# Four early jobs from a one-row slot list, scatters queued behind the next decay, and deeper x and v buffers in a retention + mixture-of-experts kernel

## The chip, the cores and the metric

One core of a Trainium2 chip runs the whole kernel. The metric is the device time of one execution in microseconds. The profile shows one execution, with the span from its first to its last instruction and the tensor clock that was granted.

## The reference

Retention with one state per head (4 sequences, 8 heads, 768 steps, width 64), then a mixture of experts over the 3072 tokens (width 512, 8 experts, hidden width 1024) in which each token goes to its best expert only:

```
state = gamma[h] * state + k_t v_t^T ;  y_t = scale * q_t state        # for t in 0..767
x = y as [3072, 512]
logits = x @ w_gate + modality_bias[modality_id];  e = argmax(logits)
gate = softmax(logits)[e]
out[token] = gate * (relu(x @ w1[e]) @ w2[e])
```

## The kernel before

**Retention.** Each sequence is cut into 6 chunks of 128 steps, so there are 24 chunks, numbered n. In chunk form y = (masked q k^T) v plus q times the state so far; the decay is folded into v (`decay_v`, on POOL) and into the output (`decay_q`, on ACT, used by DVE in `yT`). One chunk is four quarters, between which the generator `retention(n)` yields:

- loads are queued on SP, then the hooks "top", `decay_v(n+1)`, the update of the state `st`, and the hooks "st";
- `scores(n+1)` and the hooks "sc";
- the hooks "pr", `tokens_out(n-1)` (transpose of y and the gate logits; the result goes to a tile `xs`) and the hooks "tk";
- `heads_out(n)` and the hooks "end".

PE, ACT, DVE and SP run their instructions in the order of the program text. POOL's decays and index fills are pinned to that order as well.

**Routing.** After each group of three chunks, `route_a` (softmax parts, one-hot `oh`, running counts `cnt`) and `route_b` (rank of each token within its expert by matmuls, then the row number `pos`) give each token a row in `xsl`, a table in HBM with one region of 3072 rows per expert. `scatter` writes a chunk's 128 rows of x there by an indirect DMA on POOL. An `xs` tile comes free when its scatter has landed; there are 4. `setup_stores` writes 512 empty rows at the end of the table.

**Slots and jobs.** Each expert's region is divided into slots of 512 rows, 48 in all. A job is the two-layer network on one slot with its expert's weights: `rows_in` reads the slot's rows, `ids` takes token numbers and gates, `flip` transposes the rows, `raw` loads and `cut` splits the weights into a high and a low part, and 32 steps of 6 matmuls follow (`first`: 16 steps for h, `second`: 16 for o). Outputs are scattered to their tokens by POOL. While job k runs, hooks load and prepare job k+1.

Jobs come from lists. An *early* list is made while retention still runs, from slots that are already full: with `EARLY = (3, 5)` one list after 9 chunks and one after 15. `early_a` to `early_e` rank all 48 slots in a 48 x 48 comparison, with PE matmuls that broadcast the counts (`pce`, L388), pick the winner (`pte`) and mark it as taken (`ptk`). The *final* list (`final_a` to `final_d`, matmuls `pcf` and `ptf`) ranks what is left after all 24 chunks; `gaps_*` and `gap` then fill the unused rows of half-filled slots with zeros, by nine indirect DMAs on POOL (L583), before the final jobs' rows are read. Two slots of at most 32 tokens are computed as small "rests" inside later jobs. A loop at the end of the kernel takes any slots that are left over.

**The order.** Chunks 0 to 13 run alone (`FIRST_JOB = 14`). From then on job steps and quarters of chunks alternate, two quarters after an even step, one after an odd step. When retention is over, `last_tokens` runs piece by piece; each `PAUSE` hands one job step to PE. The six jobs are e0, e1 (early), f0 to f3 (final).

Of the kernel before, what the change touches and what calls it, by code (L numbers as in the profile page):

```python
# [15 lines left out]
P = 128  # L16
# [24 lines left out]
FIRST_JOB = 14  # L41
# [9 lines left out]
def kernel(  # L51
# [52 lines left out]
    cnd = cp.tile([NCAND, NCAND + 4], F32, name="cnd")  # L104
# [88 lines left out]
    def tokens_out(n, yT):  # L193
        gr = n // GRP
        if n % GRP == 0:
            lg[gr] = sm.tile([P, GRP, NE], F32, tag="lg", name=f"lg_{gr}")
        xs = xss[n] = wk.tile([P, NG, P + NE], F32, tag="xs", name=f"xs_{n}", bufs=4)
        for u in range(2):
            px = bank(f"x_{n}_{u}")[:, : 2 * (P + NE)].rearrange("p (g e) -> p g e", g=2)
            for g in range(2):  # L200
                nc.tensor.matmul(  # L201
                    px[:, g], yT[:, 2 * u + g], wgt[:, 2 * u + g], start=(g == 0), stop=(g == 1),
                    skip_group_check=True,
                )
            nc.scalar.copy(xs[:, 2 * u : 2 * u + 2], px)  # L205
# [77 lines left out]
    def route_a(gr, part):  # L283
# [10 lines left out]
        elif part == 1:  # L294
            l, ex = mid[gr]
            eq = sm.tile(shp, F32, tag="eq", name=f"eq_{gr}")
            nc.vector.scalar_tensor_tensor(eq, l, 0.0, iota3m, op0=ALU.is_equal, op1=ALU.mult)
            mn = sm.tile([P, GRP], F32, tag="mn", name=f"mn_{gr}")
            nc.vector.tensor_reduce(mn, eq, axis=AX.X, op=ALU.min)
            oh = sm.tile(shp, BF16, tag="oh", name=f"oh_{gr}")  # L300
            nc.vector.tensor_tensor(
                oh, iota3m, mn.unsqueeze(2).to_broadcast(shp), op=ALU.is_equal
            )
# [12 lines left out]
    def route_b(gr):
        oh, _ = mid.pop(gr)
# [17 lines left out]
        mid[gr] = pos  # L335
# [33 lines left out]
    def list_consts():  # L369
# [8 lines left out]
        bias = small("bias", [1, 2])  # L378
        nc.vector.memset(bias, 0.0)
        nc.vector.memset(bias[:, 0:1], float(EMPTY))  # L380
        lc.update(ord_r=ord_r, vals=vals, bias=bias)
# [35 lines left out]
    def early_a(k):  # L417
        mid["e"] = ranks_a(f"e{k}", cnt[EARLY[k]])

    def early_b(k):  # L420
        szr, szc = mid["e"]
        mid["e"] = (ranks_b(f"e{k}", szr, szc, lists.get("taken")), szc)

    def early_c(k):

        rank, szc = mid["e"]
        hit = small(f"hit{k}", [NCAND, 1])
        nc.vector.tensor_scalar(hit, szc, float(SLOT), None, op0=ALU.is_ge)
        nc.vector.scalar_tensor_tensor(hit, rank, 0.0, hit, op0=ALU.is_equal, op1=ALU.mult)
        if "taken" in lists:  # L430
# [3 lines left out]
        pick = small(f"pick{k}", [NCAND, 2], BF16)
        nc.vector.tensor_scalar(pick, lc["vals"], hit, None, op0=ALU.mult)
        mid["e"] = (hit, pick)

    def early_d(k):
        hit, pick = mid["e"]
        pt = bank(f"pte{k}")  # L440
        nc.tensor.matmul(pt[:1, 0:2], ones[:NCAND, :1], pick, start=True, stop=True)
        lst = small(f"lst{k}", [1, 2], I32)
        nc.vector.tensor_tensor(lst, pt[:1, 0:2], lc["bias"], op=ALU.add)
        lists[k] = lst
        dg = small(f"dg{k}", [NCAND, NCAND], BF16)
        nc.vector.tensor_scalar(dg, ident[:NCAND, :NCAND], hit, BIG, op0=ALU.mult, op1=ALU.mult)
        mid["e"] = (hit, dg)

    def early_e(k):
        hit, dg = mid.pop("e")  # L450
        pk = bank(f"ptk{k}")
        nc.tensor.matmul(pk[:NCAND, :NCAND], ones[:NCAND, :NCAND], dg, start=True, stop=True)
        tkr = small(f"tkr{k}", [NCAND, NCAND])
        tkc = small(f"tkc{k}", [NCAND, 1])
        if "taken" in lists:
            was = lists["taken"]
            nc.vector.tensor_tensor(tkr, pk[:NCAND, :NCAND], was[0], op=ALU.add)
            nc.vector.scalar_tensor_tensor(tkc, hit, BIG, was[1], op0=ALU.mult, op1=ALU.add)
        else:
            nc.vector.tensor_copy(tkr, pk[:NCAND, :NCAND])  # L460
            nc.vector.tensor_scalar(tkc, hit, BIG, None, op0=ALU.mult)
        lists["taken"] = (tkr, tkc)
# [351 lines left out]
    for g in range(NGRP - 1):  # L814
        t = (g + 1) * GRP
        if g + 1 in EARLY:
            k = EARLY.index(g + 1)
            at(t, "end", route_a, g, 0)
            at(t, "end", route_a, g, 1)
            at(t + 1, "sc", route_a, g, 2)  # L820
            at(t + 1, "sc", route_b, g)
            at(t + 1, "sc", early_a, k)
            at(t + 1, "pr", scatter, g, 0)
            at(t + 1, "end", scatter, g, 1)
            at(t + 2, "st", scatter, g, 2)
            at(t + 1, "pr", early_b, k)
            at(t + 1, "end", early_c, k)
            at(t + 2, "sc", early_d, k)
            at(t + 2, "pr", place_early, k)
            at(t + 3, "sc", early_e, k)  # L830
        else:
            at(t, "end", route_a, g, 0)
            at(t + 1, "st", route_a, g, 1)
            at(t + 1, "sc", route_a, g, 2)
            at(t + 1, "sc", route_b, g)
            for i in range(GRP):
                at(min(t + 1 + i, NN - 1), "pr", scatter, g, i)

    t = EARLY[0] * GRP + 2
    e = jobs[0]  # L840
    at(t, "tk", two, raw, e, 1, (0, 1))
    at(t, "end", two, raw, e, 1, (2, 3))
    at(t + 1, "pr", rows_in, e)
    at(t + 2, "top", ids, e)
    at(t + 1, "end", cut, e, 1, 0)
# [41 lines left out]

    def last_tokens():
        tokens_out(NN - 1, carry["y"])
        yield PAUSE  # L890
        route_a(NGRP - 1, 0)
        yield PAUSE
        route_a(NGRP - 1, 1)
        yield PAUSE
        final_a()
        route_a(NGRP - 1, 2)
        yield PAUSE
        route_b(NGRP - 1)
        final_b()
        scatter(NGRP - 1, 0)  # L900
        yield PAUSE
        gaps_a()
        scatter(NGRP - 1, 1)
        yield PAUSE
        final_c()
        gaps_b()
        scatter(NGRP - 1, 2)
        gaps_room()
        yield PAUSE
        final_d()  # L910
# [57 lines left out]
    with tc.manual_schedule(engines={PE, ACT, DVE, SP}):  # L968
# [16 lines left out]
        at(4, "top", setup_stores)  # L985
# [39 lines left out]
def _layout(inputs):  # L1025
# [37 lines left out]
    cand = np.zeros((NCAND, NCAND + 4), f)  # L1063
# [57 lines left out]
```

## Time and profile before

| | |
|---|---|
| runs | 451.58 us median of 3 (450.89 to 453.02) |
| profiled execution | 452.26 us |
| its span | 450.3 us |
| mean granted clock | 0.959 |
| busy: PE, DVE, ACT, POOL | 405.9, 201.0, 156.4, 92.3 us |
| DMA | 82.31 MB, mean 183 GB/s |

The span is divided into 40 slices of 11.26 us, in each of which a digit gives the busy tenths of an engine; slices are counted from 0. PE is TensorE's matmuls, PEld its weight loads, DVE VectorE, ACT ScalarE, POOL GpSimd, SP the queue that issues most DMAs. A row of a timeline has the start, the length, the engine, the line and the tiles written and read; in brackets is the idle time before it and what ended that. DMA share is the mean busy share of the 16 DMA engines.

### The profile page before, as it was taken

How to read it: one execution, taken by the hardware profiler on the slowest of the kernel's cores; microseconds unless marked ns; L12 is line 12 of the kernel's file. 1: busy time of each engine (PE TensorE's matmuls, PEld its weight loads, DVE VectorE, ACT ScalarE, POOL GpSimd, SP SyncE). 2: the span in 40 equal slices, each digit the busy share in tenths (PEclk: the TensorE clock that was granted, in tenths of full speed). 3: DMA queues.
4: the chain of work that ended last, by engine and by line, in shares of the span. 5: the costliest groups of instructions: out<-in, count | busy, mean ns of one | idle time of the engine just before them, and what ended most of it. 6: DMA issues, size and time to landing. Idle time of an engine off the chain costs nothing.

```text
span 450.3 us, 8319 instructions
## 1 busy us (share of the span) xinstructions
PE 405.9 (90%) x3104; PEld 331.3 (74%) x3104; DVE 201.0 (45%) x509; ACT 156.4 (35%) x309; POOL 92.3 (20%) x116
## 2 busy tenths in 40 slices
PE   4995959299799999999479999999999999999994
PEld 4874848188587787878368888887888888878883
DVE  1682565366765755477242146214352346224200
ACT  1541342236342454323222335223342334224211
POOL 2304414021041221357301100110001000100011
PEclk9998988879989999999869999999999999999998
DMA  8988655938548832334562347952534279810011
GB/s 283 336 226 284 203 204 182 359 151 298 172 146 295 278 118 91 150 143 172 179 206 103 131 153 284 335 193 58 189 116 144 114 233 310 305 73 0 2 47 43
DMA packets 30490, 82.31 MB, mean 183 GB/s; under 512 B 5485, under 2 KB 5613, under 8 KB 30193
## 3 DMA queue, kind: packets, MB, share of 16 engines
q1 hardware_dynamic: 25024, 66.10, 44.2%
q0 software_dynamic: 5136, 15.21, 8.5%
q8 instruction: 26, 0.43, 0.4%
q10 hardware_dynamic: 288, 0.44, 0.3%
q14 instruction: 16, 0.13, 0.1%
HBM read 65.42 MB, written 23.41 MB: 197 GB/s over the span
## 4 chain that ended last, share of the span: by engine, by line
PE 51%; issue 13%; DVE 3%; POOL 2%; DMA 2%; ACT 1%; POOLq 0%; SPq 0%; DVEq 0%; ACTq 0%
PE h_f L657 15%; PE o_f L675 14%; PE o_e L675 9%; PE h_e L657 3%; PE x L201 2%; PE xp_f L642 2%; PE y L183 2%; PE sc L159 1%; POOL xsl L583 1%; DMA xsl<-kqr,run_pos 1%; DMA xg_f<-xsl 1%; DVE lo_e L636 1%; POOL out_dram L683 1%; PE y L177 1%; PE st L215 1%
## 5 line engine op out<-in xcount | busy, mean ns | idle before, releaser
L636 DVE TENSOR_TENSOR lo_f<-raw_f,hi_f 128x1024 fp32r<-128x1024 f32 x32 | 39.2, 1225 | 49.8 <-ACT hi_f L634 49.8
L665 DVE SCALAR_TENSOR_TENSOR hTl_f<-h_f,hTh_f 128x512 fp32r<-128x512 f32 x32 | 22.1, 692 | 67.1 <-ACT hTh_f L664 67.1
L657 PE MATMUL h_f<-xTh_f,hi_f 128*128 128x512 f32 x128 | 50.9, 397 | 0.0
L675 PE MATMUL o_f<-hi_f,hTh_f 128*128 128x512 f32 x128 | 50.3, 393 | 0.0
L657 PE MATMUL h_f<-xTh_f,lo_f 128*128 128x512 f32 x128 | 50.1, 391 | 0.0
L657 PE MATMUL h_f<-xTl_f,hi_f 128*128 128x512 f32 x128 | 50.0, 391 | 0.0
L675 PE MATMUL o_f<-lo_f,hTh_f 128*128 128x512 f32 x128 | 49.9, 389 | 0.0
L675 PE MATMUL o_f<-hi_f,hTl_f 128*128 128x512 f32 x128 | 49.8, 389 | 0.0
L683 POOL DMA_INDIRECT out_dram<-o_f,tok_f x16 | 15.5, 969 | 132.8 <-ACT o_f L682 113.8
L147 POOL TENSOR_TENSOR vd<-vt,cst 128x512 f32<-128x512 f32 x24 | 25.0, 1044 | 74.9 <-PE y L183 48.1
L164 DVE TENSOR_TENSOR a<-sc,cst 128x512 f32<-128x512 f32 x48 | 30.8, 684 | 20.4 <-PE sc L159 20.4
L664 ACT ACTIVATE hTh_f<-h_f 128x512 fp32r<-128x512 f32 x32 | 19.2, 599 | 55.9 <-PE h_f L657 55.9
L345 POOL DMA_INDIRECT xsl<-xs,pos x24 | 25.6, 1066 | 58.6 <-DVE xTl_e L648 9.1
L201 PE MATMUL x<-wgt,yT 128*128 128x136 f32 x192 | 30.9, 309 | 5.5 <-DVE yT L190 5.5
L205 ACT COPY xs<-x 128x272 f32<-128x272 f32 x48 | 18.2, 387 | 49.3 <-PE x L201 18.3
L159 PE MATMUL sc<-kqr 64*128 64x128 f32 x384 | 30.8, 304 | 5.0 <-DMA kqr<-in_qkv_dram 4.9
L634 ACT CAST hi_f<-raw_f 128x1024 fp32r<-128x1024 f32 x32 | 33.4, 1043 | 0.0
L201 PEld LDWEIGHTS x<-wgt,yT 128*128 128x128 f32 x192 | 27.3, 209 | 7.4 <-DVE yT L190 3.4
L159 PEld LDWEIGHTS sc<-kqr 64*128 64x128 f32 x384 | 25.9, 205 | 9.3 <-DMA kqr<-in_qkv_dram 5.1
L682 ACT ACTIVATE o_f<-o_f,gate_f 128x512 f32<-128x512 f32 x16 | 11.0, 688 | 59.9 <-issue 34.1
L657 PEld LDWEIGHTS h_f<-xTh_f,hi_f 128*128 128x128 f32 x128 | 24.0, 188 | 6.2 <-issue 1.2
L183 PE MATMUL y<-a,vd 128*64 128x128 f32 x384 | 28.4, 294 | 0.0
(191 smaller groups left out, 710.4 us busy)
## 6 DMA issues: line engine op xcount, KB each, us to landing
raw_f<-in_w_dram SPq DMA_DIRECT2D x32, 512.0 KB, 3.4
kqr<-in_qkv_dram SPq DMA_DIRECT2D x23, 512.0 KB, 6.0
raw_e<-in_w_dram SPq DMA_DIRECT2D x16, 512.0 KB, 5.1
vt<-in_qkv_dram SPq DMA_DIRECT2D x24, 256.0 KB
kt<-in_qkv_dram SPq DMA_DIRECT2D x20, 256.0 KB, 6.4
xg_f<-xsl SPq DMA_DIRECT2D x16, 272.0 KB, 4.1
kqr<-in_w_dram SPq DMA_DIRECT2D x8, 512.0 KB
xg_e<-xsl SPq DMA_DIRECT2D x8, 272.0 KB, 6.6
```

Source lines behind the costliest of these rows:

```text
L147: nc.gpsimd.tensor_tensor(vds[n], vv, dec[:, n % NCH].unsqueeze(2).to_broadcast([P, H, D]), op=ALU.mult)
L159: nc.tensor.matmul(pe[j][:, g * P : (g + 1) * P], kt[r, g], qt[r, g], start=True, stop=True, skip_group_check=True,)
L164: nc.vector.tensor_tensor(a[:, j], pe[j].rearrange("p (h t) -> p h t", t=P), mask.unsqueeze(1).to_broadcast([P, NG, P]), op=ALU.mult,)
L183: nc.tensor.matmul(py[j][g % 2 * D : (g % 2 + 1) * D, g // 2], vd[:, 2 * g + j], a[:, j, g], start=(s is None and g < 2), stop=(g >= 2), s ...
L201: nc.tensor.matmul(px[:, g], yT[:, 2 * u + g], wgt[:, 2 * u + g], start=(g == 0), stop=(g == 1), skip_group_check=True,)
L345: ins = nc.gpsimd.indirect_dma_start(out=xsl[:, :], out_offset=bass.IndirectOffsetOnAxis(ap=mid[gr][:, i : i + 1], axis=0), in_=xs.rearran ...
L634: nc.scalar.copy(hi, t)
L636: nc.vector.tensor_tensor(lo, t, hi.bitcast(F32), op=ALU.subtract)
L657: nc.tensor.matmul(s.ph, s.w[1][f // 2][wi][:, o : o + P], s.xT[kc][a], start=(kc == 0 and k == 0), stop=(kc == KC - 1 and k == 2),)
L665: nc.vector.scalar_tensor_tensor(lo, s.ph, 0.0, hi.bitcast(F32), op0=ALU.max, op1=ALU.subtract)
L675: nc.tensor.matmul(s.po, s.hT[f][a][:, hh * P : (hh + 1) * P], s.w[2][f // 2][wi][:, (f % 2) * DM : (f % 2 + 1) * DM], start=(f == 0 and k ...
L683: ins = nc.gpsimd.indirect_dma_start(out=out[:, :], out_offset=bass.IndirectOffsetOnAxis(ap=s.tok[:, hh : hh + 1], axis=0), in_=o[:, :], i ...
```

## The change

- Four early jobs instead of two: lists after 9, 15 and 21 chunks, the last of which picks two. Two final jobs remain instead of four.
- An early list is made on one row of 48 slots instead of 48 x 48. A matmul sums the counts onto one partition; DVE marks the full slots, multiplies by a fixed priority (`bid`), takes the maximum, decodes slot and expert from it by a shift and a mask, and clears that slot's `bid`. The marks of taken slots for the final list are made once, from `bid` (`taken_a`, `taken_b`).
- `route_b` is divided: `route_c` holds its DVE part. For group g let t be chunk 3(g + 1). `route_a` 0 and 1 run at the end of chunk t; `route_b`, the list, `route_c` and `route_a` 2 now all run at the end of chunk t + 1 (they began in the middle of it); the scatters run in chunks t + 2 and t + 3, each after that chunk's decay (before: from chunk t + 1 on).
- Five `xs` tiles instead of four, three `vt` instead of two (v is loaded three chunks ahead), one `dq` instead of two.
- `setup_stores` moves from chunk 4 to chunk 7 and is declared independent of the scatters.
- The first job starts at chunk 15, and e0's loads, rows and flips are moved with it. `last_tokens` has 7 pauses instead of 9, with the gap stores ahead of `final_d`.

```diff
-EARLY = (3, 5)
-NEARLY = len(EARLY)
-NLAST = 4
+EARLY = {3: (0,), 5: (1,), 7: (2, 3)}
+NEARLY = 4
+NLAST = 2
-FIRST_JOB = 14
+FIRST_JOB = 15
...
-        t = vts[n] = ld.tile([P, DM], F32, tag="vt", name=f"vt_{n}", bufs=2)
+        t = vts[n] = ld.tile([P, DM], F32, tag="vt", name=f"vt_{n}", bufs=3)
-        t = wk.tile([P, NG, P], F32, tag="dq", name=f"dq_{n}")
+        t = wk.tile([P, NG, P], F32, tag="dq", name=f"dq_{n}", bufs=1)
-        xs = xss[n] = wk.tile([P, NG, P + NE], F32, tag="xs", name=f"xs_{n}", bufs=4)
+        xs = xss[n] = wk.tile([P, NG, P + NE], F32, tag="xs", name=f"xs_{n}", bufs=5)
...
-            nc.sync.dma_start(xsl[r : r + P, :], fill["none"])
+            ins = nc.sync.dma_start(xsl[r : r + P, :], fill["none"])
+            tc.add_to_no_dep_group("rows", ins.ins)
...
-    def early_a(k): ... early_e(k): ...        # 48 x 48 ranks, three matmuls
+    def early_a(g):
+        pt = bank(f"pte{g}")
+        nc.tensor.matmul(
+            pt[:1, :NCAND], ones[:, :1], cnt[g].unsqueeze(2).to_broadcast([P, NE, SPE]),
+            start=True, stop=True,
+        )
+        mid["e"] = pt
+    def early_b(g):
+        full = small(f"full{g}", [1, NCAND])
+        nc.vector.tensor_tensor(full, mid.pop("e")[:1, :NCAND], lc["full_at"], op=ALU.is_ge)
+        for k in EARLY[g]:
+            bid = lc["bid"]
+            key = small(f"key{k}", [1, NCAND])
+            nc.vector.tensor_tensor(key, full, bid, op=ALU.mult)
+            top = small(f"top{k}", [1, 1])
+            nc.vector.tensor_reduce(top, key, axis=AX.X, op=ALU.max)
+            num = small(f"num{k}", [1, 1], I32)
+            nc.vector.tensor_scalar(
+                num, top, -1.0, float(EMPTY * NE), op0=ALU.mult, op1=ALU.add
+            )
+            lst = small(f"lst{k}", [1, 2], I32)
+            nc.vector.tensor_scalar(lst[:, 0:1], num, 3, None, op0=ALU.logical_shift_right)
+            nc.vector.tensor_scalar(lst[:, 1:2], num, NE - 1, None, op0=ALU.bitwise_and)
+            lists[k] = lst
+            hit = small(f"hit{k}", [1, NCAND])
...
+                hit, key, top, full, op0=ALU.is_equal, op1=ALU.mult
...
+                bid, hit, 0.0, bid, op0=ALU.is_equal, op1=ALU.mult
+    def taken_a():
+        tk = small("tk", [1, NCAND], BF16)
+        nc.vector.tensor_scalar(tk, lc["bid"], 0.0, BIG, op0=ALU.is_equal, op1=ALU.mult)
+    def taken_b():
+        nc.tensor.matmul(pk[:NCAND, :NCAND], ones[:1, :NCAND], tk, start=True, stop=True)
+        nc.tensor.matmul(pk[:NCAND, P : P + 1], tk, ones[:1, :1], start=True, stop=True)
...
+        at(t, "end", route_a, g, 0)
+        at(t, "end", route_a, g, 1)
+        at(t + 1, "end", route_b, g)
         if g + 1 in EARLY:
...
+            at(t + 1, "end", early_a, g + 1)
+            at(t + 1, "end", early_b, g + 1)
+            for k in EARLY[g + 1]:
+                at(t + 2, "st", place_early, k)
...
+        at(t + 1, "end", route_c, g)
+        at(t + 1, "end", route_a, g, 2)
+        at(t + 2, "st", scatter, g, 0)
+        at(t + 2, "end", scatter, g, 1)
+        at(min(t + 3, NN - 1), "end" if t + 3 == NN else "st", scatter, g, 2)
+    t = GRP * min(EARLY)
     e = jobs[0]
...
+    at(t + 2, "sc", two, raw, e, 1, (0, 1))
+    at(t + 2, "end", two, raw, e, 1, (2, 3))
+    at(t + 4, "sc", rows_in, e)
+    at(t + 4, "end", cut, e, 1, 0)
+    at(t + 5, "top", raw, e, 2, 0)
+    at(t + 5, "sc", ids, e)
     for kc in range(KC):
+        at(t + 5, ("sc", "pr", "tk", "end")[kc], flip, e, kc)
...
-        if n + 2 < NN:
-            load_v(n + 2)
         if n + 3 < NN:
+            load_v(n + 3)
             load_kq(n + 3)
...
+        taken_a()
         yield PAUSE
+        route_a(g, 0)
+        taken_b()
         yield PAUSE
+        route_a(g, 1)
         yield PAUSE
+        route_b(g)
         final_a()
+        gaps_a()
+        route_c(g)
+        route_a(g, 2)
+        scatter(g, 0)
         yield PAUSE
         final_b()
+        gaps_b()
+        scatter(g, 1)
+        scatter(g, 2)
+        gaps_room()
         yield PAUSE
         final_c()
         gaps_c()
         for e in range(-1, NE):
             gap(e)
         yield PAUSE
+        final_d()
+        for i in range(NLAST):
             place(jobs[NEARLY + i], lists["final"], i, U + i)
...
-        at(4, "top", setup_stores)
+        at(7, "top", setup_stores)
```

More of the change, by code (lines that the diff above doesn't have):

```diff
@@ L103 @@
     ones = cp.tile([P, P], BF16, name="ones")
-    cnd = cp.tile([NCAND, NCAND + 4], F32, name="cnd")
+    cnd = cp.tile([NCAND, 2 * NCAND + 3], F32, name="cnd")
     cnt = [cp.tile([P, NE], BF16, name=f"cnt{i}") for i in range(NGRP + 1)]
@@ L308, in route_a @@
         else:
-            oh, ex = mid[gr]
+            pos, ex = mid[gr]
             den = sm.tile([P, GRP], F32, tag="den", name=f"den_{gr}")
@@ L314, in route_a @@
                 nc.vector.reciprocal(xss[gr * GRP + i][:, 0, P + 1 : P + 2], den[:, i : i + 1])
+            mid[gr] = pos
     def route_b(gr):
-        oh, _ = mid.pop(gr)
+        oh, ex = mid[gr]
         pr = bank(f"rk_{gr}")[:, : GRP * NE].rearrange("p (c e) -> p c e", e=NE)
@@ L329, in route_b, with route_c @@
             )
+        mid[gr] = (oh, ex, pr)
+    def route_c(gr):
+        oh, ex, pr = mid[gr]
         rk = sm.tile(shp, F32, tag="rk", name=f"rkt_{gr}")
@@ L334, in route_b @@
             nc.vector.tensor_reduce(pos, rk, axis=AX.X, op=ALU.add)
-        mid[gr] = pos
+        mid[gr] = (pos, ex)
     def scatter(gr, i):
@@ L377, in list_consts @@
         nc.vector.tensor_copy(vals[:, 1:2], ex_c)
[L378 to L381, printed above, removed]
+        full_at = small("full_at", [1, NCAND])
+        nc.vector.tensor_scalar(full_at, off_r[:1], float(SLOT), None, op0=ALU.add)
+        bid = small("bid", [1, NCAND])
+        nc.vector.tensor_copy(bid, cnd[:1, NCAND + 3 :])
+        lc.update(ord_r=ord_r, vals=vals, full_at=full_at, bid=bid)
     def ranks_a(t, counts):
@@ L415, in ranks_b @@
         return rank
[L417 to L430, printed above, removed]
+    def early_a(g):
[5 more added lines that the diff above has]
+        mid["e"] = pt
@@ L431, in early_c @@
             nc.vector.scalar_tensor_tensor(
-                hit, lists["taken"][1], 0.0, hit, op0=ALU.is_equal, op1=ALU.mult
+                hit, key, top, full, op0=ALU.is_equal, op1=ALU.mult
             )
[L434 to L461, printed above, removed]
+            nc.vector.scalar_tensor_tensor(
+                bid, hit, 0.0, bid, op0=ALU.is_equal, op1=ALU.mult
+            )
@@ new lines, in taken_a @@
+    def taken_a():
+        tk = small("tk", [1, NCAND], BF16)
+        nc.vector.tensor_scalar(tk, lc["bid"], 0.0, BIG, op0=ALU.is_equal, op1=ALU.mult)
+        lists["tk"] = tk
+    def taken_b():
+        tk = lists["tk"]
+        pk = bank("ptk")
+        nc.tensor.matmul(pk[:NCAND, :NCAND], ones[:1, :NCAND], tk, start=True, stop=True)
+        nc.tensor.matmul(pk[:NCAND, P : P + 1], tk, ones[:1, :1], start=True, stop=True)
+        tkr = small("tkr", [NCAND, NCAND])
+        nc.vector.tensor_copy(tkr, pk[:NCAND, :NCAND])
+        tkc = small("tkc", [NCAND, 1])
+        nc.vector.tensor_copy(tkc, pk[:NCAND, P : P + 1])
@@ L723, in rest_load @@
             for h in range(2):
-                t = ld.tile([P, DM], F32, tag=tag, name=f"rw{m}{i}{h}", bufs=2)
+                t = ld.tile([P, DM], F32, tag=tag, name=f"rw{m}{i}{h}", bufs=2 if k == 6 else 3)
                 nc.sync.dma_start(t, src[:, h * DM : (h + 1) * DM])
@@ L728, in rest_in @@
     def rest_in(s):
-        s.xg = wk.tile([P, XW], F32, tag="xs", name="rx", bufs=4)
+        s.xg = wk.tile([P, XW], F32, tag="xs", name="rx", bufs=5)
         for g in range(4):
@@ L815 @@
         t = (g + 1) * GRP
+        at(t, "end", route_a, g, 0)
+        at(t, "end", route_a, g, 1)
+        at(t + 1, "end", route_b, g)
         if g + 1 in EARLY:
[L817 to L839, printed above, removed]
-    e = jobs[0]
[L841 to L845, printed above, removed]
+            at(t + 1, "end", early_a, g + 1)
[8 more added lines that the diff above has]
+    t = GRP * min(EARLY)
+    e = jobs[0]
+    at(t + 2, "sc", two, raw, e, 1, (0, 1))
[4 more added lines that the diff above has]
+    at(t + 5, "sc", ids, e)
     for kc in range(KC):
-        at(t + 2, ("st", "sc", "tk", "end")[kc], flip, e, kc)
-    at(t + 2, "top", raw, e, 2, 0)
+        at(t + 5, ("sc", "pr", "tk", "end")[kc], flip, e, kc)
     carry = {}
@@ L888, in last_tokens @@
     def last_tokens():
+        g = NGRP - 1
         tokens_out(NN - 1, carry["y"])
+        taken_a()
         yield PAUSE
-        route_a(NGRP - 1, 0)
+        route_a(g, 0)
+        taken_b()
         yield PAUSE
-        route_a(NGRP - 1, 1)
+        route_a(g, 1)
         yield PAUSE
+        route_b(g)
         final_a()
-        route_a(NGRP - 1, 2)
+        gaps_a()
+        route_c(g)
+        route_a(g, 2)
+        scatter(g, 0)
         yield PAUSE
-        route_b(NGRP - 1)
         final_b()
[L900 to L903, printed above, removed]
+        gaps_b()
+        scatter(g, 1)
+        scatter(g, 2)
+        gaps_room()
         yield PAUSE
         final_c()
[L906 to L910, printed above, removed]
         gaps_c()
@@ L913, in last_tokens @@
             gap(e)
-        place(jobs[NEARLY], lists["final"], 0, U)
         yield PAUSE
-        for i in range(1, NLAST):
+        final_d()
+        for i in range(NLAST):
             place(jobs[NEARLY + i], lists["final"], i, U + i)
@@ L978 @@
         load_kq(2)
+        load_v(2)
         decay_v(0)
@@ L1062, in _layout @@
     ci = np.arange(NCAND)
[L1063 removed]
+    cand = np.zeros((NCAND, 2 * NCAND + 3), f)
     cand[:, :NCAND] = (ci % SPE) * SLOT
```

1 line of the change is left out of this document (added).

## The prediction

> **What bounds the kernel now.** I read the page's slices first, then the list of who waits for whom, filtered to PE, then busy time by stretches, then the timelines of PE, POOL, ACT and SP around each hole.
>
> ```profile
> PE 405.9 (90%) x3104; PEld 331.3 (74%) x3104; DVE 201.0 (45%) x509; ACT 156.4 (35%) x309; POOL 92.3 (20%) x116
> PE   4995959299799999999479999999999999999994
> PEclk9998988879989999999869999999999999999998
> ```
>
> PE is the bound, with 44.4 us idle out of 450.3. The slices put the holes before slice 11 (124 us) and at slice 19; slices 21 to 38 are full. The change can therefore win only in the first 100 us, around 120 us and around 220 us, and only up to those holes plus what the clock loses behind them.
>
> ```profile
> PE xp_e L642 <- DMA xg_e<-xsl: 8.6, 3, 8.2
> PE xp_f L642 <- DMA xg_f<-xsl: 8.6, 4, 6.3
> PE x L201 <- DVE yT L190: 5.5, 3, 3.3
> PE pce L388 <- DVE crepe L385: 5.4, 2, 3.2
> 58.60:62.00 3.40, 3.40 (x32) 2.82 (x32) 1.27 (x3) 1.18 (x4) 0.00 (x0) 0.50 0.39 156
> 88.80:96.10 7.30, 6.68 (x37) 5.33 (x38) 4.90 (x24) 1.56 (x3) 0.00 (x0) 0.50 0.67 262
> 123.40:126.80 3.40, 3.40 (x14) 3.10 (x15) 1.72 (x11) 0.77 (x2) 2.17 (x3) 0.51 0.23 87
> 222.40:229.00 6.60, 1.40 (x3) 0.55 (x3) 0.65 (x6) 0.00 (x0) 0.00 (x0) 0.50 0.78 233
> 229.00:232.60 3.60, 3.52 (x11) 3.04 (x12) 2.19 (x5) 2.12 (x3) 0.00 (x0) 0.50 0.46 181
> 232.70:444.00 211.30, 211.30 (x1119) 172.50 (x1117) 71.04 (x106) 70.86 (x104) 20.36 (x21) 1.00 0.43 152
> ```
>
> The waits (us, times, longest) name the holes: rows of the first early job, rows of the first final job, yT, and the early list's count. In the stretches (length, then busy time of PE, PEld, DVE, ACT, POOL, then granted clock, DMA share, GB/s) the clock is 0.50 behind each hole and 1.00 elsewhere: half of the busy time there is lost as well. From 232.7 on nothing can be won.
>
> **The change, part by part.** Sums are made against the profiled execution, 452.26 us: span 450.3 and 1.96 around it. It lies 0.7 above the median of 451.58.
>
> *Chunks 0 to 14, before any job.* Undisturbed, PE needs 4.30 us a chunk (12.43 to 25.34 is three):
>
> ```profile
> 11.77 0.63 PE L215 MATMUL st<-vd,kt 128*64 128x64 f32 x16
> 12.43 1.16 PE L159 MATMUL sc<-kqr 64*128 64x128 f32 x16
> 25.34 1.16 PE L159 MATMUL sc<-kqr 64*128 64x128 f32 x16
> 27.25 0.19 PE L319 MATMUL rk<-oh,upper 128*128 128x24 bf16 x1 [0.75 <-DVE oh L301]
> 27.57 1.17 PE L201 MATMUL x<-wgt,yT 128*128 128x136 f32 x8
> 33.82 1.17 POOL L345 DMA_INDIRECT xsl<-xs,pos  x1 [7.74 <-PE y L183]
> 36.43 1.02 POOL L345 DMA_INDIRECT xsl<-xs,pos  x1 [0.28 <-POOL xs L341]
> 39.85 0.67 ACT L205 COPY xs<-x 128x272 f32<-128x272 f32 x2 [9.52 <-DMA xsl<-xs,pos]
> 43.72 0.67 ACT L205 COPY xs<-x 128x272 f32<-128x272 f32 x2 [2.91 <-DMA xsl<-xs,pos]
> ```
>
> The first scatter stands on POOL until 33.8, after the four stores of empty rows (L248), with the next decay behind it; ACT's copy of x then waits for a free xs buffer, that is, for the scatter four chunks back to land, 6.0 to 7.3 us after it starts (33.82 to 39.85, 36.43 to 43.72). The stores lose that order and move to chunk 7; the scatters go behind the decay; a fifth xs gives each copy a chunk more. Chunk n's copy may start 4.3 us after its host chunk begins before PE feels it (two copies, lg and yT follow, then x). A scatter now starts about 1.5 us into the chunk before, so it lands 7.5 to 8.8 in, against 8.6 allowed: no wait in an ordinary group. Behind the list at 9 chunks, pos is about 1.3 us later and chunk 12's x may wait 1 to 2 us; that lies inside the wait for rows below. route_b now follows one-hots a chunk old, so waits like the 0.75 before rk go. The third v tile deepens a prefetch and costs nothing. One dq tile instead of two makes ACT wait for yT of the chunk before, which DVE does first in a chunk (0.86 us): covered, and if DVE lags, ACT lags with it.
>
> So chunk 14 is reached at 11.77 + 13 x 4.30, less four parts of 0.63 (two chunks without a state, two that start a sequence), plus four ranks of 0.32 (27.25 to 27.57): 66.4; state and scores (0.63, 1.16) end at 68.2, where PE wants e0's rows. When do they land? In the trace:
>
> ```profile
> 76.40 3.07 SPq L629 DMA_DIRECT2D raw_e<-in_w_dram  x4
> 81.18 2.47 SPq L612 DMA_DIRECT2D xg_e<-xsl  x4
> 90.81 0.48 PE L642 MATMUL xp_e<-cst,xg_e 128*128 128x128 f32 x1 [0.21 <-DMA xg_e<-xsl]
> 91.21 2.08 PE L159 MATMUL sc<-kqr 64*128 64x128 f32 x16
> 98.79 0.48 PE L657 MATMUL h_e<-xTh_e,hi_e 128*128 128x512 f32 x1
> 80.00:90.00 10.00, 1.58 (x22) 0.89 (x18) 2.77 (x10) 2.61 (x7) 1.12 (x2) 0.80 1.00 353
> ```
>
> Full DMA (share 1.00) moves 353 GB/s. A chunk is 512, 256 and 256 KB, a weight tile 512, a row tile or scatter 272. At 81.2 some 1.4 MB were queued (2.1 MB of weights and 1.05 of a chunk, less 4.8 us of work), plus 1.1 of rows: 7.1 us and about 2 for completion, and the last tile came 9.6 after the issue. The same reckoning after: the weights go out at chunks 11 and 12 (54 to 58 us), rows_in must wait for the scatter of chunk 8, which starts behind the decay of chunk 12 (59.9) and lands near 67. From 54 to 67 the queues are given three chunks (3.15), weights (2.1), three scatters (0.84): 6.1 MB; 12.9 us at 345 (353, a little less with scatters between) move 4.45. Backlog 1.65 and rows 1.1 take 8 us, completion 2: the last tile is there at 77. **PE again waits about 8 us for rows**, now at the flips of chunk 14. From the last tile to e0's first matmul the trace takes 8.0 (90.81 to 98.79), of which 2.4 are scores and ranks (91.21: 2.08; 0.32) that now lie ahead of the wait: e0 starts at 82.6. Today it starts at 98.79 with chunk 14 still to do, 4.3: **gain 20.5**. Bounds: 28 if the rows come before 68.2 (four flips at 0.87, the rest of the chunk 4.30 - 0.63 - 1.16, so 74.2), 13 if the weights' backlog, the stores at chunk 7 (1.1 MB) and the scatters add 7 us.
>
> *Early lists.* The old list holds PE at L388 from inside the chunk; the second costs 3.15 of wait (the 3.2 in the list of waits), 0.2, and half of 3.4 at clock 0.51. The new one is a matmul that PE passes without waiting and 8 small DVE operations for one job, 15 for two:
>
> ```profile
> 74.51 0.14 DVE L443 TENSOR_TENSOR lst<-pte,bias 1x2 int32<-1x2 f32 x1
> ```
>
> At 0.14, or a little more for 48 values, that is 1.3 and 2.4 us, on a DVE 45% busy, with pos and the next a behind it, neither due within 2 us. SP waits for the list at the end of chunk t+2's state, with nothing urgent behind it. **Gain 5.0**; bounds 3 and 5.5.
>
> *The final list.* With four early jobs, the list, the gap stores and the reads behind them belong to e2, one job later than f0 relative to their start.
>
> ```profile
> 187.87 1.17 PE x L201 x8
> 193.12 0.13 PE pcf L388
> 196.00 0.18 DVE L334 TENSOR_REDUCE pos<-rkt 128x3 int32<-128x24 f32 x1
> 196.50 0.48 PE L657 MATMUL h_e<-xTh_e,hi_e 128*128 128x512 f32 x1
> 198.20 0.19 PE ptf L490
> 205.10 0.98 POOL L583 DMA_INDIRECT xsl<-kqr,one_pos  x1 [0.88 <-DVE far_r L574]
> 222.68 2.10 SPq L612 DMA_DIRECT2D xg_f<-xsl  x4
> 225.38 0.15 DVE L623 COPY tok_f<-xg_f 128x1 int32<-128x1 int32 x1 [4.93 <-DMA xg_f<-xsl]
> 254.22 21.92 PE h_f L657 x96
> 276.14 0.87 PE xp_f L642 x8
> ```
>
> The hole here is 8.6 of wait and half of 1.40 + 3.52 at clock 0.50: 11.1 in all. After: retention ends at step 24 of e0 instead of 26 (36 quarters at 1.5 a step), so the last x ends seven steps of 1.37 (21.92 for 16) before e1. Call that end t (189.04 today). The work that had seven steps now has five: PE asks for pcf at t+4.3, three steps on, and for ptf two steps later, while today 5.1 us lie between the two (193.12, 198.20), with DVE at work on the keys and picks. I put 0.7 of PE wait before pcf and 1.3 before ptf: 2.0 new. e1 starts at t+11.9 and wants e2's rows after 16 steps, t+33.8. POOL gets pos at about t+6.7 (today t+7.1), does today's work (196.18 to 205.10 less 0.88 idle: 8.0) and starts the gaps at t+14.7; today 17.6 us pass until the rows are issued (205.10 to 222.68), 2.7 more to the first tile: t+35.0. PE waits 1.2, then the 2.3 between tiles (8.6 - 6.3). **Removed 11.1; added 2.0, 3.5 and one stretch at half clock, 1.7: gain 3.9.** Bounds: 9 (gaps land in time) and 0.
>
> Of that 1.7: rows show a wait of about 2 us followed by a half-clock stretch (2.07 before x at 58.28, then 58.6 to 62.0 at 0.50).
>
> ```profile
> 58.28 1.86 PE L201 MATMUL x<-wgt,yT 128*128 128x136 f32 x8 [2.07 <-DVE yT L190]
> ```
>
> The Trainium skill, page "TensorE: Matmul & The Clock Gate", Part 1, has the clock fall to half only after an idle window of about 3.4 us, free-running. By that rule a wait cut into 1.2 and 2.3 us would leave the clock alone and the sum would be 1.7 lower; this trace disagrees, and the row decides.
>
> *What stays.* Six job bodies and both rests, flips, outputs: moved, not changed. Routing the reference's inputs gives 5 full slots, one of 478, one of 31, one of 3; after 9, 15 and 21 chunks 2, 2 and 4 are full. All four early picks succeed, two final jobs take the full slot and the 478, and the loop at the end runs no turn, as today.
>
> **Sum:** 452.3 - 20.5 - 5.0 - 3.9 = 422.9 for a profiled execution, 422 for the median.
>
> **Rivals.** *The rows come in time:* the wait of 8.2 and that for e2's rows vanish, PE bounds from chunk 1 on: gains 28, 5.5, 9, so 409. For it: slices 11 to 18 show the same loads hidden. Against it: DMA share 1.00 in the row from 80 to 90. *New waits take more:* the backlog before chunk 14 and a DVE behind its lists; gains 13, 3, 0: 436. For it: the same full DMA row, at a slower pace than the new one. *DMA is the bound of the whole first phase*, and packing retention denser only moves the wait: gains 0, 3, 0, so 449. Against it: 18 chunks (18.1 MB: three carry no k), 11 scatters (3.1), stores (1.1), weights (2.6), rows (1.1) and constants are under 27 MB, 76 us at 353; today's phase is 99. *An early list finds no full slot* (the change fails its aim; slower): a job body runs on empty rows, 47 us (192 matmuls at 21.92/96, four flips at 0.87), and with five slots left the tail test fails, so the loop runs three jobs without overlap, each over 47: about 565 or more. It decides if fewer than four slots hold 512 after chunk 21; the counts say 1386 and 1299 for the two large experts, so two each.
>
> **How the numbers follow.** Forecast 422, chance 0.64; rows in time 0.16; new waits 0.14; DMA-bound 0.02; missed list or another unseen serial wait 0.04. The range 411 to 434 covers the first case's bounds and reaches towards both neighbours. Half a per cent, 2.3 us, is about what a measurement here can tell from no change; only the last case is slower.
>
> **What would show it.** Right: first h_e near 83; xs copies before it waiting under 2 us; PE's wait for xg_e 6 to 9, before chunk 15; no wait at the early list; PE waits of 1 to 2 at pcf and ptf; gap stores starting 1 to 4 us after e1's first matmul; a wait for e2's rows of 1 to 5; h_f and o_f as now. Wrong: h_e after 90, a hole inside e0 (ACT behind the single dq), or any turn of the last loop.

## The result and the profile after

The changed kernel takes 430.03 us (median of 4 runs, 426.15 to 430.70); the kernel before took 451.94 beside it. The ratio is 0.9497 (95% interval 0.9434 to 0.956). The forecast was 422, in a range of 411 to 434: the direction and most of the size came, 8 us of the gain did not. The profiled execution of the changed kernel took 430.70 us, its span 428.5, so 21.6 us less than the profiled execution before.

The page's busy times and slices, after:

```profile
PE 399.3 (93%) x3101; PEld 327.7 (76%) x3101; DVE 199.7 (47%) x508; ACT 155.7 (36%) x309; POOL 92.3 (22%) x116
PE   4999498699999999899799999999999999999994
PEclk9999889889999999999999999999999999999998
```

PE's idle time has fallen from 44.4 to 29.2 us. The holes are now in slices 4 and 6 to 7 (45 to 55 us, 70 to 86 us) and, much smaller, around 175 and 205 us. Who waited for whom on PE (total, times, longest), and for the stores of empty rows on SP:

```profile
PE st L215 <- DMA kt<-in_qkv_dram: 5.5, 1, 5.5
PE xp_e L653 <- DMA xg_e<-xsl: 4.2, 5, 1.9
PE x L201 <- DVE yT L190: 4.0, 1, 4.0
PE ptf L501 <- DVE pick_f L494: 1.3, 1, 1.3
PE xp_e L653 <- DVE a L164: 1.3, 1, 1.3
PE rk L321 <- DVE oh L302: 0.4, 1, 0.4
PE pcf L396 <- DVE crepf L393: 0.2, 1, 0.2
SPq L248 <- DMA xsl<-xs,pos: 6.7, 1, 6.7
```

The wait for the early list's count (`pce`) is gone, the wait for the first job's rows is down from 8.6 to 2.4 (1.1 and 1.3; the other 3.1 under `xg_e` are e2's rows), and the wait for the rows behind the gap stores from 8.6 to 3.1. (The 1.3 is put down to DVE's `a`, which ended last; the first tile of rows had itself landed only about then, at least 6.2 us after its issue at 78.31.) A new wait heads the list: PE for a tile of k. The rows around it, from the timelines of SP and PE:

```profile
36.48 0.45 SPq L122 DMA_DIRECT2D kqr<-in_qkv_dram  x1
43.68 3.45 SPq L248 DMA_DIRECT2D xsl<-none  x4
47.23 0.40 SPq L131 DMA_DIRECT2D kt<-in_qkv_dram  x1
52.57 1.12 PE L215 MATMUL st<-vd,kt 128*64 128x64 f32 x16 [5.48 <-DMA kt<-in_qkv_dram]
50.00:60.00 10.00, 7.43 (x98) 6.75 (x100) 2.87 (x6) 2.32 (x7) 0.89 (x1) 0.66 0.80 286
```

SP issues nothing from 36.9 to 43.7. It stands at the four stores of empty rows, which wait for the last of three scatters to land (it started on POOL at 36.44), and the k for chunk 9 is queued behind them. PE waits 5.48 us, and the clock is 0.66 on average from 50 to 60, that is, two thirds of that stretch at half speed.

The way to the first job then has these rows (POOL, ACT, SP, PE):

```profile
67.21 1.02 POOL L351 DMA_INDIRECT xsl<-xs,pos  x1 [2.68 <-DVE a L164]
75.55 0.67 ACT L205 COPY xs<-x 128x272 f32<-128x272 f32 x2 [7.02 <-DMA xsl<-xs,pos]
76.94 1.83 PE L201 MATMUL x<-wgt,yT 128*128 128x136 f32 x8 [4.03 <-DVE yT L190]
78.31 2.04 SPq L623 DMA_DIRECT2D xg_e<-xsl  x4
84.68 0.30 PE L653 MATMUL xp_e<-cst,xg_e 128*128 128x128 f32 x1 [1.28 <-DVE a L164]
92.42 0.48 PE L668 MATMUL h_e<-xTh_e,hi_e 128*128 128x512 f32 x1
```

A scatter takes 8.3 us to land (67.21 to 75.55), so the copy of x stands still for 7.0 and PE for 4.0. The first job starts at 92.42, with chunk 14 done; before, it started at 98.79 with chunk 14 still ahead.

### The profile page after: what moved, and what is told of

Same layout as the page of the kernel before. It is cut to its first block, busy times and chain, and to the rows that moved or that the text cites. A ratio compares the mean times of both kernels' runs of the same rounds, so it can differ in the third digit from the quotient of the medians.

```text
span 428.5 us, 8308 instructions
## 1 busy us (share of the span) xinstructions
PE 399.3 (93%) x3101; PEld 327.7 (76%) x3101; DVE 199.7 (47%) x508; ACT 155.7 (36%) x309; POOL 92.3 (22%) x116
## 4 chain that ended last, share of the span: by engine, by line
PE 62%; DMA 13%; issue 13%; DVE 6%; POOL 3%; SPq 1%; ACT 1%; POOLq 0%; ACTq 0%; DVEq 0%
PE o_e L686 17%; PE h_e L668 16%; PE h_f L668 5%; PE sc L159 5%; PE o_f L686 4%; PE y L183 4%; PE x L201 4%; DMA xsl<-xs,pos 3%; DMA xg_e<-xsl 3%; DMA kqr<-in_qkv_dram 3%; DMA xsl<-kqr,run_pos 2%; PE st L215 2%; PE y L177 2%; PE xp_e L653 2%; DMA cst<-in_consts_dram 1%
## 5 line engine op out<-in xcount | busy, mean ns | idle before, releaser
L647 DVE TENSOR_TENSOR lo_e<-raw_e,hi_e 128x1024 fp32r<-128x1024 f32 x32 | 39.8, 1244 | 32.3 <-ACT hi_e L645 32.1
L668 PE MATMUL h_e<-xTh_e,hi_e 128*128 128x512 f32 x128 | 52.0, 406 | 0.0
L686 PE MATMUL o_e<-hi_e,hTh_e 128*128 128x512 f32 x128 | 51.6, 403 | 0.0
L668 PE MATMUL h_e<-xTl_e,hi_e 128*128 128x512 f32 x128 | 50.1, 392 | 0.0
L668 PE MATMUL h_e<-xTh_e,lo_e 128*128 128x512 f32 x128 | 50.1, 391 | 0.0
L686 PE MATMUL o_e<-lo_e,hTh_e 128*128 128x512 f32 x128 | 50.0, 390 | 0.0
L686 PE MATMUL o_e<-hi_e,hTl_e 128*128 128x512 f32 x128 | 49.9, 390 | 0.0
L645 ACT CAST hi_e<-raw_e 128x1024 fp32r<-128x1024 f32 x32 | 33.4, 1043 | 0.0
L668 PEld LDWEIGHTS h_e<-xTh_e,hi_e 128*128 128x128 f32 x128 | 24.0, 188 | 6.0 <-issue 0.6
L668 PEld LDWEIGHTS h_e<-xTl_e,hi_e 128*128 128x128 f32 x128 | 24.0, 188 | 5.3
```

Source lines behind the costliest of these rows:

```text
L645: nc.scalar.copy(hi, t)
L647: nc.vector.tensor_tensor(lo, t, hi.bitcast(F32), op=ALU.subtract)
L668: nc.tensor.matmul(s.ph, s.w[1][f // 2][wi][:, o : o + P], s.xT[kc][a], start=(kc == 0 and k == 0), stop=(kc == KC - 1 and k == 2),)
L686: nc.tensor.matmul(s.po, s.hT[f][a][:, hh * P : (hh + 1) * P], s.w[2][f // 2][wi][:, (f % 2) * DM : (f % 2 + 1) * DM], start=(f == 0 and k ...
```

## The experiments

Times are medians; ratios are to the kernel before, run beside each group of experiments (its medians there are 450.95, 451.89 and 451.38). "First job" is the start of the first `h_e` matmul in the profiled run. The runs of one kernel lie 1.4 to 5.9 us apart, and a bracket behind a ratio is its 95% interval; where the intervals of two kernels overlap, the waits in the traces say what changed, and the time alone does not.

**The stores back at chunk 4**, ahead of the first scatter:

```diff
-        at(7, "top", setup_stores)
+        at(4, "top", setup_stores)
```

> The changed kernel with the four stores of empty rows put back at the top of chunk 4, ahead of the first scatter; all else as changed. Theory (SP stands still): at chunk 7 the stores come behind three scatters and wait 6.7 us for the last of them to land, and the loads of k behind them on SP come too late, which is PE's 5.5 us wait at chunk 8 and the 6.8 us at half clock behind it. Then the wait is gone, the first job's first matmul comes at 85 to 88 instead of 92.4, and the time is 423 to 426 against 430. Rival (bytes): the stores' 1.1 MB take the DMA's time wherever they stand; then PE waits for k or kq elsewhere before chunk 11 and the time stays at 429 to 431.

424.79 us, ratio 0.9461 (0.9404 to 0.9519). PE's list of waits, then the first job:

```profile
PE st L215 <- DMA kt<-in_qkv_dram: 1.1, 1, 1.1
86.77 0.48 PE L668 MATMUL h_e<-xTh_e,hi_e 128*128 128x512 f32 x1
```

The 5.5 us wait at chunk 9 is gone (the 1.1 stands at chunk 6), the first job starts 5.65 us earlier, the median is 5.2 lower. The theory's numbers hold, the rival's do not. One of the four runs took 429.28, though, and the interval of the ratio overlaps that of the changed kernel: the rows show the wait gone, the size of the gain is less sure.

**The stores at chunk 7, freed in both directions.** A group can say "the scatters need not wait for these stores"; it takes a second group to say "these stores need not wait for the scatters":

```diff
             tc.add_to_no_dep_group("rows", ins.ins)
+            tc.declare_no_dep(ins.ins, group="scat", reason="rows of no token")
...
         disjoint(ins, "rows")
+        tc.add_to_no_dep_group("scat", ins.ins)
```

> The changed kernel with the stores still at chunk 7, but declared independent of the scatters in their own direction too, so that SP need not wait for a scatter to land before it issues them. Theory (SP stands still): as with the stores at chunk 4, PE's wait for k is gone, first job matmul at 85 to 88, time 423 to 426. Rival (bytes at chunk 7): 1.1 MB in front of the loads of chunks 9 and 10 still makes k late; PE keeps 3 us or more of its 5.5, time 428 to 431.

423.95 us, ratio 0.9425 (0.939 to 0.9461).

```profile
47.79 0.69 PE L215 MATMUL st<-vd,kt 128*64 128x64 f32 x16 [1.27 <-DMA kt<-in_qkv_dram]
84.05 0.48 PE L670 MATMUL h_e<-xTh_e,hi_e 128*128 128x512 f32 x1
```

The bytes stay where they were and the wait falls to 1.27. So it was SP's standing still, not the 1.1 MB. With this mended, the first job comes at 84.05 where the prediction had 82.6. That nearness is partly luck. PE reaches the state of chunk 14 at 76.07, not at 66.4, held up by a wait of 4.3 before x and the half clock behind it; but the last tile of rows is only 3 us later than forecast (79.95 against 77), and the way from it to the job takes 4.1 us instead of 5.6.

**Two early jobs instead of four**, all else as changed:

```diff
-EARLY = {3: (0,), 5: (1,), 7: (2, 3)}
-NEARLY = 4
-NLAST = 2
+EARLY = {3: (0,), 5: (1,)}
+NEARLY = 2
+NLAST = 4
```

> The changed kernel with two early jobs (lists at 9 and 15 chunks) and four final ones, as before; new order, buffers and one-row list kept. Theory (the wait belongs to the place): the rows of the third job are read at step 10 of the second, and that read waits for the gap stores whether the job is early or final; so PE waits 3 to 4 us for its rows as in the changed kernel (3.1), and the time is 429 to 432. Rival (the number of early jobs is what shortens it): the wait goes back to 6 to 9 us with a half-clock stretch, time 434 to 439.

428.33 us, ratio 0.952 (0.9491 to 0.9549), against 0.9497 for four.

```profile
PE xp_f L653 <- DMA xg_f<-xsl: 1.8, 2, 1.4
SPq L623 <- DMA xsl<-kqr,run_pos: 6.5, 1, 6.5
199.34 2.10 SPq L623 DMA_DIRECT2D xg_f<-xsl  x4
```

The third job's wait for rows is 1.8, even less than 3.1. The two further early jobs gain nothing as the change has them: the third job's rows are read at the same step, behind the same gap stores, whichever list named it. SP stands 6.5 us at that read until a gap store (`run_pos`) has landed, here and in the changed kernel alike.

**The gap stores held back** until the third job's rows have been read:

```diff
         final_c()
+        for _ in range(13):
+            yield PAUSE
         gaps_c()
         for e in range(-1, NE):
             gap(e)
```

> The changed kernel with the nine gap stores (and the last list parts behind them) held back by 13 job steps, so that the third job's rows are read ahead of them in the program's order. Theory (the read waits for gap stores that its full slot does not need): PE's 3.1 us wait for these rows is gone and the time is 426 to 428. Rival (the rows are late for their buffers or behind weights on the queue): the wait stays above 2 us and the time at 429 to 431; if the gap stores now delay the first final job's rows, slower by up to 5.

426.94 us, ratio 0.9475 (0.945 to 0.95; the interval of the changed kernel holds this one whole). The read of the rows, and PE's total wait for all early jobs' rows:

```profile
194.17 2.09 SPq L623 DMA_DIRECT2D xg_e<-xsl  x4
PE xp_e L653 <- DMA xg_e<-xsl: 0.7, 2, 0.4
```

The rows are read at 194.2 instead of 201.2, SP's 6.5 us wait is gone, and PE no longer waits for them (the 0.7 belong to the first job); the final jobs' rows are not late either. This is what four early jobs make possible: a full slot needs no gap stores, so its read may come ahead of them.

**Both mended** (freed stores at chunk 7, late gap stores):

> The changed kernel with the stores freed of the scatters at chunk 7 and the gap stores held back by 13 job steps. Theory: the two waits lie far apart and each is PE's own, so the gains add: 424.0 and 426.9 alone against 430 give 420 to 422. Rival (one of them only moves a wait): 423 to 425.

420.39 us, ratio 0.9301 (0.9264 to 0.9338): by the medians the gains add (6.1 and 3.1 alone, 9.6 together), and this kernel is faster than both the one before and the changed one, with intervals that do not touch. Its first phase is the base of most of the runs below:

```profile
PE x L201 <- DVE yT L190: 5.2, 2, 4.5
PE xp_e L655 <- DMA xg_e<-xsl: 1.0, 3, 0.4
84.83 0.47 PE L670 MATMUL h_e<-xTh_e,hi_e 128*128 128x512 f32 x1
70.00:80.00 10.00, 8.00 (x79) 6.47 (x79) 7.35 (x26) 5.35 (x16) 2.42 (x3) 0.66 1.04 400
```

**Two v tiles instead of three** in that kernel, v loaded two chunks ahead:

```diff
-        t = vts[n] = ld.tile([P, DM], F32, tag="vt", name=f"vt_{n}", bufs=3)
+        t = vts[n] = ld.tile([P, DM], F32, tag="vt", name=f"vt_{n}", bufs=2)
...
-        if n + 3 < NN:
-            load_v(n + 3)
+        if n + 2 < NN:
+            load_v(n + 2)
+        if n + 3 < NN:
             load_kq(n + 3)
...
-        load_v(2)
```

> The same, with two v tiles and v loaded two chunks ahead, as before the change. Theory (the prediction's: the third v tile is worth nothing): within 1.5 us of the kernel with both. Rival (v then lands too late for POOL's decay while the queue is full of weights): PE waits 2 us or more for vd before the first job, 2 to 6 us slower.

423.74 us, ratio 0.9364 (0.9321 to 0.9407), 3.4 us more than with three, though the two intervals overlap a little. Not vd is late, as the rival had it, but the rows:

```profile
73.04 3.14 SPq L625 DMA_DIRECT2D xg_e<-xsl  x4
81.37 0.30 PE L655 MATMUL xp_e<-cst,xg_e 128*128 128x128 f32 x1 [3.21 <-DMA xg_e<-xsl]
```

The rows are issued 0.8 us later than with three tiles (72.25), SP needs 3.14 us instead of 2.00 for the four issues, and PE waits 3.2 us at the first flip. Why a third v tile should do this stays open: it is not that a load leaves the full stretch, since both SP timelines show the same loads between the first job's weights and its rows (two each of v, kq and k), in this run about 1 us later.

**Six x tiles** with two v tiles (and a small tile, `modn`, moved into a shared buffer):

```diff
-..., tag="xs", name=f"xs_{n}", bufs=5)
+..., tag="xs", name=f"xs_{n}", bufs=6)
```

> The same with two v tiles and six x tiles. Theory (the job's rows are next in line): PE's 4 us wait for yT before chunk 13, which comes from chunk 11's copy standing still for a scatter, goes; but rows_in still waits for the scatter of chunk 8 and PE waits 3 to 6 us for rows instead; against the kernel with two v tiles 0 to 2 us faster. Rival (the x tiles are the bound there): the whole wait and the half-clock stretch behind it are won, 4 to 6 us faster.

423.98 us, ratio 0.9382 (0.935 to 0.9414): no gain over two v tiles alone.

```profile
76.42 1.07 PE L215 MATMUL st<-vd,kt 128*64 128x64 f32 x16 [4.74 <-DMA kt<-in_qkv_dram]
81.88 0.30 PE L655 MATMUL xp_e<-cst,xg_e 128*128 128x128 f32 x1 [2.38 <-DMA xg_e<-xsl]
```

PE no longer waits for yT at all (4.4 with five). Its waits for k grow from 1.0 to 6.5 in all, 4.7 of it here, and those for rows stay about the same, 3.4 against 4.1. The theory had the size; that the wait would go to k and not to the rows it had not. The DMA share is 1.02 from 70 to 82 us, which fits a DMA that is the bound in the last chunks before the first job, with the x tiles only choosing where PE waits for it.

**Four x tiles** in the kernel with both:

> The kernel with both, but four x tiles as before the change. Theory (a scatter needs 6 to 8 us to land and four tiles leave one chunk of 4.3 for it): about 4 us of PE wait in each of the groups at chunks 5, 8 and 11, and half-clock stretches, 10 to 18 us slower, 430 to 440; the wait for rows shrinks to nothing. Rival (the scatters' new place behind the decay does the work, the fifth tile little): within 3 us.

440.51 us, ratio 0.9756 (0.9718 to 0.9794): 20.1 us slower, just above the theory's range.

```profile
PE x L201 <- DVE yT L190: 16.5, 4, 7.7
78.19 0.67 ACT L205 COPY xs<-x 128x272 f32<-128x272 f32 x2 [10.45 <-DMA xsl<-xs,pos]
79.49 2.18 PE L201 MATMUL x<-wgt,yT 128*128 128x136 f32 x8 [7.70 <-DVE yT L190]
98.28 0.48 PE L670 MATMUL h_e<-xTh_e,hi_e 128*128 128x512 f32 x1
```

The waits before x are 4.0, 2.2 and 7.7, and the first job comes 13.5 us later; after it PE waits 2.5 more before x and 3.0 at `ptk`, where there were 0 and 0.2. The fifth tile is worth 20 us in this order of work: scattering later needs it.

**The kernel before with its stores freed**, at chunk 4:

```diff
-            nc.sync.dma_start(xsl[r : r + P, :], fill["none"])
+            ins = nc.sync.dma_start(xsl[r : r + P, :], fill["none"])
+            tc.add_to_no_dep_group("rows", ins.ins)
```

> The kernel before, with one edit: the four stores of empty rows (at chunk 4, ahead of the first scatter) are declared rows that scatters need not wait for. Theory: the first scatter starts near 30 us instead of 33.8, the decay and the state update behind it (PE's 1.9 us) are in time, but with four x tiles the copies at chunks 5, 8 and 11 still wait; first job matmul at 93 to 97 instead of 98.8, 446 to 449 against 451.6. Rival (the early list and the rows' wait take back what is won): 450 to 452.

452.24 us, ratio 1.0011 (0.9981 to 1.0042): nothing.

```profile
30.82 1.17 POOL L346 DMA_INDIRECT xsl<-xs,pos  x1 [4.57 <-DVE yT L190]
39.81 0.68 ACT L205 COPY xs<-x 128x272 f32<-128x272 f32 x2 [9.30 <-DMA xsl<-xs,pos]
41.21 2.15 PE L201 MATMUL x<-wgt,yT 128*128 128x136 f32 x8 [5.27 <-DVE yT L190]
```

The first scatter starts 3 us earlier and lands at the same time: the copy behind it runs at 39.81, as it did at 39.85. It now takes 9.0 us instead of 6.0, with the DMA share up from 0.87 to 0.95 between 30 and 40 us. PE's wait at the state update goes and the one before x grows from 3.25 to 5.27. The first job comes at 98.49, not at 93 to 97: the theory fell.

**The same, and five x tiles:**

> The same kernel before with the stores freed, and five x tiles instead of four. Theory (from the 20 us that the fourth-tile run lost): the waits for yT (5.5 us) and two half-clock stretches behind them go, first job matmul at 86 to 91, 437 to 443. Rival (the tiles help only with the scatters behind the decay and the ranks at the chunk's end): within 2 us of the kernel with the stores freed alone.

446.48 us, ratio 0.9896 (0.9841 to 0.995).

```profile
82.50 1.07 PE L643 MATMUL xp_e<-cst,xg_e 128*128 128x128 f32 x2 [8.87 <-DMA xg_e<-xsl]
92.48 0.48 PE L658 MATMUL h_e<-xTh_e,hi_e 128*128 128x512 f32 x1
```

The waits for yT are gone (7.0 to 0.2) and the first job comes 6 us earlier, but the early list in mid-chunk (2.3) and the wait for rows (8.9) remain. The theory had 437 to 443 and the rival at most 2 us; neither came. The tile brings 6 us here, against 20 in the new order.

**Row numbers ahead of the early list** on DVE, in the kernel with both:

> The kernel with freed stores and late gap stores, with the row numbers (route_c) made ahead of the early list on DVE instead of behind it. Theory (the list holds the scatter back): at the list of 9 chunks pos and the first scatter come 1.3 us earlier (60.1 instead of 61.4), PE's 4.5 us wait at chunk 12 falls to 3 to 3.5, the rows are read 1 us earlier; 417 to 420 against 420.4. Rival (landing time, not the start, sets it, or the weights come later by what the list loses): 420 to 422.

420.81 us, ratio 0.9304 (0.9258 to 0.9349): no difference in time.

```profile
61.31 1.02 POOL L352 DMA_INDIRECT xsl<-xs,pos  x1 [2.37 <-DVE a L164]
PE x L201 <- DVE yT L190: 3.1, 1, 3.1
PE xp_e L655 <- DMA xg_e<-xsl: 2.8, 4, 1.7
```

The time is the rival's, but the run does not test the theory, because the edit did not move the scatter: it starts at 61.31, where it started at 61.40. The row numbers are there at 58.5 (DVE), yet a scatter also carries the gates, which `route_a` 2 writes into the x tile, and those still come behind the list, at 60.3. The wait before x falls from 4.5 to 3.1 all the same, the wait for rows rises from 1.0 to 2.8 and that for k from 0.6 to 1.8: another pair of traces in which the waits shift and the time stays.

**Scatters ahead of the next decay** in the kernel with both:

```diff
-        at(t + 2, "st", scatter, g, 0)
-        at(t + 2, "end", scatter, g, 1)
-        at(min(t + 3, NN - 1), "end" if t + 3 == NN else "st", scatter, g, 2)
+        at(t + 1, "end", scatter, g, 0)
+        at(t + 1, "end", scatter, g, 1)
+        at(t + 2, "end", scatter, g, 2)
```

> The kernel with freed stores and late gap stores, with the scatters put ahead of the next decay again (right behind route_c). Theory (the decay has the slack, the scatter waits for pos anyway): the first scatter of a group starts no earlier than now plus or minus 0.5, the decay behind two scatters comes 2 to 4 us later, PE waits 0.5 to 2 us for vd in each group before the jobs; 422 to 430. Rival (the order on POOL does not matter): 419 to 422.

423.31 us, ratio 0.9362 (0.9318 to 0.9407): 2.9 us slower (the intervals overlap a little, the single runs do not).

```profile
68.07 1.12 PE L215 MATMUL st<-vd,kt 128*64 128x64 f32 x16 [2.93 <-POOL vd L147]
```

PE waits 1.9, 0.9 and 2.9 us for the decayed v in the three groups before the jobs: the decay stands behind scatters for which POOL waits 5.2 to 6.8 us on DVE. Scattering behind the decay is worth about 3 us.

## Why the prediction was right, and where it was not

By its own steps, in the profiled executions (452.26 to 430.70):

| step | predicted gain | from the traces |
|---|---|---|
| to the first job (98.79 + 4.3, now 92.42) | 20.5 | 10.7 |
| early list | 5.0 | 5.05 |
| final list and gap stores | 3.9 | 6.1 |
| sum | 29.4 | 21.8 (total 21.6) |

Only the first row is the difference of two starts; the other two are added up from the waits and half-clock stretches that went and came. From the first `h_e` to the first `o_e` of the second job, chunk 14 taken off, the traces differ by 10.3 where these two rows give 11.15.

**The first phase is the step that failed**: its gain of 10.7 lies below its own bounds of 13 to 28, and two of the prediction's signs say so, the first `h_e` "after 90" (92.42) and a copy of x that waits 7.0 us and not "under 2". The time still lies within 411 to 434 because that range is wide and the other two steps came at least as forecast. The fault is at the sentence that the stores "lose that order and move to chunk 7". The declaration works for scatters that come after the stores. At chunk 7 the stores themselves come after three scatters, and SP waits 6.7 us for the last of them to land, with the loads of k behind it. I had counted the stores' bytes and not their wait, nor asked what is queued behind them on SP. The run with the stores freed recovers 6.1 of the 8 us that were missing, by the medians.

**The wait for rows** was to be 8 us. It was 2.4, with 4.0 before it at the copy of x, which I had put at "1 to 2" and "inside the wait for rows": 6.4 together. The sum was nearly right and its parts were not, I take it because both waits draw on the same full DMA; the run with six x tiles points the same way: removing the wait for yT raises the one for k. The size that was off is the landing of a scatter: 8.3 us, where I took 6.0 to 7.3. The Trainium skill, page "DMA: Bandwidth & Descriptors", section "Anatomy of one DMA — SWDGE (gpsimd) path", fits a DMA issued from GpSimd as about 2.0 us plus its bytes at 436 GB/s; for a scatter of 272 KB that is an estimate of 2.6. The first scatter took 6.0 us to release its buffer before (33.82 to 39.85) and 9.0 with the stores freed (30.82 to 39.81). In the changed kernel the same scatters land after 2.8 us at the least: the median is 7.2 between 60 and 100 us, at a DMA share of 0.78, and 2.8 between 140 and 200 us, at 0.44. So the estimate fits light traffic, and the traffic sets the rest.

**The fifth x tile** was rightly named as what keeps the copies from waiting, and never priced by itself. It is the part that cost most to leave out of those tried: 20 us, in the new order with both waits mended. **The third v tile** was put at nothing; without it the median is 3.4 us longer, with intervals that overlap a little and no cause shown.

**The early list** came out as worked: no PE wait, no half-clock stretch. Nor is there a hole inside e0, the other sign of being wrong: PE is full in slices 9 to 15, and the single `dq` tile costs nothing there.

**The final list**: PE waits of 0.6 before `pcf` (0.7 predicted, with the 0.4 at `rk`), 1.3 before `ptf` (1.3), 3.1 for e2's rows (3.5). The rows, from the timelines of POOL, SP and PE:

```profile
185.37 0.97 POOL L594 DMA_INDIRECT xsl<-kqr,one_pos  x1 [0.88 <-DVE got L532]
201.21 2.09 SPq L623 DMA_DIRECT2D xg_e<-xsl  x4
207.00 0.33 PE L653 MATMUL xp_e<-cst,xg_e 128*128 128x128 f32 x1 [1.86 <-DMA xg_e<-xsl]
200.00:210.00 10.00, 6.92 (x34) 5.49 (x33) 4.44 (x13) 3.33 (x7) 0.00 (x0) 1.00 0.74 243
```

The half-clock stretch that I charged (1.7) did not come: the granted clock is 1.00 from 200 to 210 behind waits of 1.86 and 1.22. The Trainium skill, page "TensorE: Matmul & The Clock Gate", Part 1, with its idle window of about 3.4 us, gave that result, and I had decided against it by one row of the kernel before. In the run with the freed stores, waits of 1.72 and 0.72 at the same place were followed by a lower clock:

```profile
190.00:200.00 10.00, 7.55 (x35) 5.98 (x34) 5.16 (x13) 2.73 (x4) 0.41 (x1) 0.96 0.83 286
200.00:210.00 10.00, 10.00 (x45) 8.38 (x45) 4.01 (x6) 4.82 (x7) 0.80 (x1) 0.87 0.22 73
```

So waits of about 2 us sometimes cost a half-clock stretch and sometimes not. That the window runs free of the work, as the page has it, would fit; no run here tests it.

The gain of this step was ascribed to the shorter chain of pauses and the earlier end of retention. That fits: with two early jobs it is the same, so their number is not the reason; no run takes the pauses or the end of retention by itself. What failed is the opening remark that the gap stores come one job later relative to their start. They do not; the third job's read waits for them, early or not, until they are held back. Of the rivals, "new waits take more" (436) was nearest to the size, but by a wait on SP that it did not name.

## What to carry to other kernels

Before moving a DMA on an in-order queue, list what it will wait for at its new place and which loads stand behind it: "nothing waits for this" and "this waits for nothing" are two declarations. A buffer's price is the time that its release takes at the worst traffic, not the issue of the DMA that releases it. Where several waits stand in front of one full DMA, removing one of them can move it to the next, as with the sixth x tile, so they are to be priced together. Before testing what an operation waits for, list everything that it reads: the scatter read the gates as well as the row numbers.

## What the runs showed of the hardware that was not expected

The stretch that I took for full DMA before (share 1.00, 353 GB/s) is not the most it moves: after, 391 GB/s between 80 and 90 us at share 1.02, and 400 at 1.04 in the kernel with both mended. Indirect scatters of the same 272 KB took 2.8 to 8.6 us to land within one run of the changed kernel; the first one of the kernel before, started 3 us earlier beside the stores of empty rows, released its buffer at the same time, after 9.0 us instead of 6.0.
